# Softmax sums of ten late couples moved in front of the next couple's scores, with undivided x

## The chip, the core and the metric

The kernel runs on one core of a Trainium2 chip. The core has four engines that compute and that run beside each other, each in its own order: TensorE (PE) for matrix products, VectorE (DVE), ScalarE (ACT) and GpSimd (POOL). A fifth, SyncE (SP), issues most of the transfers. PE writes into PSUM, a small memory of eight banks; DVE and ACT empty it into SBUF, the working memory. The metric is the time of one execution on the device in microseconds (us), the median of several runs.

## What is computed

An attention block over 8 batches and 12 heads (448 rows of 64), with q and k normalised by their root mean square, and behind it a feed-forward block with a silu:

```python
q_n, k_n = (rmsnorm(q, g_q), rmsnorm(k, g_k))
scores = scale * np.matmul(q_n, k_n.transpose(0, 1, 3, 2))
scores = scores - np.max(scores, axis=-1, keepdims=True)
attn = np.exp(scores)
attn = attn / (np.sum(attn, axis=-1, keepdims=True) + 1e-09)
attn_out = np.matmul(attn, v).astype(np.float32)
...
x = np.ascontiguousarray(attn_out.transpose(0, 2, 1, 3)).reshape(B * S, H * D)
h = x @ w_in
g = h * (1.0 / (1.0 + np.exp(-h)))
return (g @ w_out).astype(np.float32)
```

All of it is in fp32. The sum of the exponentials (the softmax sum) and the product with v are independent of each other: the division may be done on the result, x.

## The kernel before

The function `bounded` holds the path that these inputs take. Work is cut into 24 couples: a couple is four heads of one batch, that is two pairs of heads, and three couples make a batch. `GROUP` is 6 (two batches), `LATE` is 9 and `SOON` is 11; `FULL` names couples 6 and 10, whose sums have an additional term. The order of all instructions is written out by hand; there is no scheduler that reorders them. Semaphores make one engine wait for another, and a tile pool makes the first writer of a buffer wait for the last reader of its former content.

For each couple c there are two stretches.

`visit(c)` computes the transposed scores of couple c, seven times four matmuls of 64 rows and 64 columns on four tiles of the PE array at once (L749). ACT takes each bank through exp into `weights` (L754). Between the scores stand the products of weights with v (`weigh`, L786): those of the last key block and of the left-over keys of couple c-1 first, then those of couple c. They accumulate in two banks, `av0` and `av1`, of which there is one buffer each. When couple c-1 is complete, `divide` (L855) multiplies each bank by the reciprocal softmax sums on DVE and writes x to SBUF. Only then can PE begin on av for couple c. `turn` (L762) is a copy of one column that orders the two halves of `weigh`; PE waits for it.

`between(c)` runs the first feed-forward product for a group of batches that is complete (`halves_in`, L955): products after Strassen and Winograd, seven for each block of 2 by 2, each of three matmuls of 128 x 128. A matmul of fp32 shows as two passes in the trace. `fill` deals them out: a call has a due number of matmuls (14 in the late couples), and other work is put between them. Items of `others` are spread evenly over the steps; items of `prompt` go in at the start and then after every third step. A between has two fills. The first one carries `late`, the adds of the couple's weights into one block (`add`, L800, on DVE) among others. Ahead of the second fill stands `sum_up`: four matmuls with a matrix of ones, on tiles of 128 rows and 32 columns (L824, eight passes), write the softmax sums into a bank. Then `prompt` holds `invert` of its left half, `invert` of its right half with `spread`, and the transposing of k (`flip`, L685, and `gain`). `invert` (L833) is a reciprocal on DVE from PSUM into `r`; `spread` copies it (L839) and lets SP issue four small transfers that exchange the halves of partitions (L842).

Banks: products take turns between the pool of `mm` (two buffers) and that of `sc` (two buffers of two banks). `sc` also serves the scores, `sum_up` from couple 6 on, and L715, a small product at the end of between whose result DVE (L716) and POOL (L719, L728) turn into the factors for q. A product that is begun in one fill can be completed in the next between; it then keeps its buffer of `mm` through the visit.

When a group of six couples is complete, its x is summed in pairs (`sum_x`), and the products of that group run in the betweens of the next six couples. The last group's products and the second feed-forward product follow after couple 23, where PE has no attention work.

Of the kernel before, what the change touches and what calls it, by code (L numbers as in the profile page):

```python
# [11 lines left out]
F32 = mybir.dt.float32  # L12
# [15 lines left out]
BANK = 512  # L28
# [514 lines left out]
def bounded(  # L543
# [3 lines left out]
    P, D, R, J, S = z.P, z.D, z.R, z.J, z.S  # L547
# [9 lines left out]
    GROUP, LATE = z.NPAIR, z.LATE  # L557
    EARLY = GROUP - 1
    SOON = 2 * GROUP - 1
    FULL = (GROUP, SOON - 1)  # L560


    hidden = dram.tile([z.NF, P, z.B * S], F32, name="hidden")
# [67 lines left out]
    def x_of(c, i):  # L631
        b, cp = divmod(c, z.NPAIR // 2)
        return xT(b, 2 * cp + i)
# [75 lines left out]
    def scale(c):  # L709

        if c >= NC:
            return
        f = norm.rms[c % 2][:, 0:n]
        t = ps.tile([P, 2, BANK], F32, name="sc", bufs=2)[:, 0, 0:n]
        nc.tensor.matmul(t, ident, f, start=True, stop=True)  # L715
        nc.vector.tensor_scalar(  # L716
            out=f, in0=t, scalar1=1.0 / D, scalar2=1e-6, op0=ALU.mult, op1=ALU.add
        )
        nc.gpsimd.tensor_tensor(out=f, in0=f, in1=minus_half.to_broadcast([P, n]), op=ALU.pow)  # L719
        if c > SOON:  # L720
            scale_rows(c, nc.gpsimd)
# [14 lines left out]
    sums = [None] * 2  # L736
# [67 lines left out]
    def sum_up(c):  # L804

        n = D // 2
        early = c < GROUP  # L810
        t = bank(S) if c < GROUP else ps.tile([P, 2, BANK], F32, name="sc", bufs=2)[:, 0, 0:S]
        terms = [(0, lambda: weights(c, 0))]
        if early:
            terms = [(0, lambda: weights(c, LEFT - 1))] + terms + [(1, None)]
        if c in FULL:
            terms.insert(0, (1, None))
        if c == GROUP - 1:
            terms.insert(1, (0, lambda: weights(c, 1)))
        for k, (which, w) in enumerate(terms):
            if early and k == len(terms) - 2:  # L820
                yield
            for h in range(2):
                for i in range(2):
                    nc.tensor.matmul(  # L824
                        t[ds(h * D + i * n, n), :],
                        ones[:, which + i if which else 0],
                        left_weights(c)[:, h] if which else w()[:, i, h],
                        start=(k == 0), stop=(k == len(terms) - 1),
                    )

        def invert(half):
            rows = ts(half, S // 2)
            nc.vector.reciprocal(out=factors(c)[0][:, rows], in_=t[:, rows])  # L833

        def spread():
            mine = [a.rearrange("(h i p) s -> i h p s", h=2, i=2) for a in factors(c)]
            queues = (nc.sync, nc.gpsimd if c == GROUP - 1 else nc.sync)
            if c >= EARLY:
                nc.vector.tensor_copy(factors(c)[1], factors(c)[0])  # L839
                for i in range(2):  # L840
                    for h in range(2):
                        queues[h].dma_start(mine[i][1 - i, h], mine[i][i, h])  # L842
                return
            for h in range(2):
                for i in range(2):
                    nc.sync.dma_start(mine[1][i, h], mine[0][1, h])
            for h in range(2):
                nc.sync.dma_start(mine[0][1, h], mine[0][0, h])

        yield [lambda: invert(0), lambda: (invert(1), spread())]  # L850

    def divide(c, source):
        for i in range(2):
            x = x_of(c, i)
            nc.vector.tensor_tensor(  # L855
                out=x, in0=x if source is None else source[i], in1=factors(c)[i], op=ALU.mult
            )
# [72 lines left out]
    def bank(n):  # L930
        turn = turns["next"] = (turns["next"] + 1) % 4
        due = filler["due"] / S
        if turns["least"] < due <= turns["most"] and not turns["aside"]:
            turns["aside"] = True
            return ps.tile([P, 2, BANK], F32, name="sc", bufs=2)[:, 0, 0:n]
        turns["aside"] = False
        if ps_alone is None or turn == 0:
            return ps_mm.tile([P, BANK], F32, name="mm")[:, 0:n]
        return ps_alone.tile([P, BANK], F32, name="alone")[:, 0:n]
# [536 lines left out]
    def visit(c):  # L1476

        beside = normalise(c + 1) if 0 < c <= GROUP else []
        if c == GROUP:
            beside = [lambda: None] + beside[2:]  # L1480
        if c < NC:
            scores(c, 0, 0)
        for step in visits.get(c, "")[:1]:
            step_of[step]()
        if c == 0:
            first_q(1)
            normalise_alone(1)
            scores(c, 1, 0)
        if c == 0:
            run_all(beside[0:1])  # L1490
        else:
            weigh(c - 1, LEFT)
            weigh(c - 1, LEFT - 1, 0)
            turn(1, nc.scalar.copy if c <= GROUP else nc.vector.tensor_copy)
            run_all(beside[0:1])
            if GROUP < c < NC and c % GROUP == 0:
                sum_x(last_two(c), 0, range(2, 4))
        if c < NC:
            scores(c, 0, 1)
        if c > 0:  # L1500
            weigh(c - 1, LEFT - 1, 1)
            if c - 1 < EARLY:
                for i in range(2):
                    nc.vector.tensor_copy(x_of(c - 1, i), sums[i])
                run_all(beside[1:2])
                if c == GROUP // 2 + 1:
                    divide(c - 2, None)
                if inverting:
                    while len(inverting) > 1:
                        inverting.pop(0)()  # L1510
                    if c > 1:
                        divide(c - 2, None)
            else:
                divide(c - 1, sums)
                if c == GROUP:
                    for i in range(1, HW):
                        sum_x(last_two(c), i, range(2))
                    for i in range(2):
                        norm.scale(c + 1, q_of(c + 1), q_of(c + 1), i, nc.vector)
                    room.w_in.round()  # L1520
                run_all(beside[1:2])
                if GROUP < c < NC and c % GROUP == 0:
                    for i in range(1, HW):
                        sum_x(last_two(c), i)
                weights_in_visit(c)
            if c + 1 < NC:
                loads["vrest"](c + 1)
        if c == NC:
            return
        if c > 0:  # L1530
            scores(c, 1, 0)
        scores(c, 1, 1)
        if c <= GROUP:
            run_all(beside[2:3])
        weigh(c, 0, 1)
        scores(c, 2, 0)
        weigh(c, 1, 1)
        turn(0, nc.scalar.copy)
        if c < GROUP:
            run_all(beside[3:4])  # L1540
        scores(c, 2, 1)
        weigh(c, 0, 0)
        if c < GROUP:
            scores(c, LEFT)
        if c != GROUP - 1:
            run_all(add(c, 1))
        weigh(c, 1, 0)
        if c < GROUP // 2:
            room.w_in.open()
        if c >= GROUP:  # L1550
            scores(c, LEFT)
        if c + 1 < NC:
            loads["v"](c + 1)
        if len(inverting) == 1:
            inverting.pop()()
# [5 lines left out]
    def between(c):  # L1561

        def transposes_and_sums():
            summing = sum_up(c)
            if c < GROUP:
                next(summing)
            if c == GROUP - 1:
                reciprocals = next(summing)
                divide(c - 1, None)
                sum_x([0, 1], 0)  # L1570
                run_all(reciprocals)
                return
            if c < LATE - 1:
                transpose_k(c + 1)
            reciprocals = next(summing)
            if LATE - 1 <= c < NC - 1:
                reciprocals += [lambda: flip(c + 1, "k"), gain]
            if GROUP // 2 < c < EARLY:
                divide(c - 1, None)
            return reciprocals  # L1580
# [28 lines left out]
        if c == GROUP:  # L1609
# [3 lines left out]
            )  # L1613
            late = third + late + fourth
        late += further[2:] if c >= GROUP else further[:2]
        if LATE - 1 <= c < SOON:
            late.insert(len(late) // 2, lambda: load_q(c + 2))
        fill(late)
# [22 lines left out]
                sum_x([c // GROUP * 2, c // GROUP * 2 + 1], 0, range(2))  # L1641
        if c >= LATE - 2:
            scale(c + 2)
        if GROUP <= c < NC - 1:

            nc.scalar.activation(first, minus_half, AF.Exp)
# [1 line left out]
            while rounder.load():  # L1648
                pass

    begun, inverting = {}, []
    load_q(2)
    for _ in range(2):
        room.w_in.load()
# [240 lines left out]
```

## Time and profile before

| what | us |
|---|---|
| median of three runs | 1301.02 |
| the three runs | 1300.94, 1302.18, 1301.02 |
| the profiled execution, by the same clock as the runs | 1300.95 |
| its span, first to last instruction | 1299.1 |
| visit of couple 15 begins, visit of couple 16 begins | 410.34, 443.77 |
| last sum (couple 23) | 699.79 |

The span by engine: PE is shown busy for 1288.5 us (99%), PE's weight loads for 833.8, DVE for 952.4, ACT for 504.0, POOL for 358.4. The groups that bear on the change, over the whole span: the number after x counts the instructions, then come the busy time in us, the mean of one in ns and the idle time of the engine just before them:

```profile
L754 ACT ACTIVATE work<-sc,rms 128x448 f32<-128x448 f32 x318 | 181.9, 635 | 84.7 <-PE sc L749 72.6
L749 PE MATMUL sc<-work 64*64 64x448 f32 x1344 | 165.0, 543 | 1.2 <-ACT work L652 0.7
L800 DVE TENSOR_TENSOR work<-work 128x896 f32<-128x896 f32 (+1 forms) x110 | 117.6, 1099 | 51.1 <-PE av L786 50.6
L786 PE MATMUL av<-work,rows 64*64 64x448 f32 x1272 | 152.3, 540 | 0.3 <-DVE av L762 0.3
```

A line names the line of the code, the engine and the operation, then what is written and what is read. `64*64` is the tile of the PE array. Ends of matmuls are modelled, so that consecutive ones overlap in the listing; starts are exact. An execution of the kernel has about 1.9 us around the span, which the runs' clock counts too.

### The profile page before, as it was taken

The page shows a single profiled execution, that of the slowest core. Times are in us where ns is not written, and L with a number is a line of the kernel's source. Part 1 is how long each engine was busy: PE and PEld are TensorE (multiplying, and loading weights), DVE is VectorE, ACT ScalarE, POOL GpSimd, SP SyncE. Part 2 cuts the span into 40 slices and gives each one's busy share as a digit, 9 for nine tenths or more (in the row PEclk, how much of TensorE's full clock was granted, in tenths as well). Part 3 has the DMA queues.
Part 4 walks back from the last instruction along what each step waited for, and adds up shares of the span by engine and source line. Part 5 has one row for each costly group of instructions (what it writes and reads, how often), then busy time and mean ns, then how long its engine had stood idle before and what let it go on. Part 6 is the DMA issues. An engine that isn't in the chain of part 4 may idle for free.

```text
span 1299.1 us, 19842 instructions
## 1 busy us (share of the span) xinstructions
PE 1288.5 (99%) x7182; PEld 833.8 (64%) x7182; DVE 952.4 (73%) x1650; ACT 504.0 (39%) x880; POOL 358.4 (28%) x221
## 2 busy tenths in 40 slices
PE   9999999999999999999999999999999999999998
PEld 4444444444444444444444455559999999999997
DVE  6899778768555557656544886698978787878785
ACT  7977566645554554544543344310000010000000
POOL 6755454443334334333311344400000000000000
PEclk9999999999999999999999999999999999999999
DMA  8675447444443444443411466312322323131411
GB/s 228 178 188 139 108 124 194 93 93 91 121 92 89 118 93 93 121 92 90 104 51 50 152 200 229 117 61 89 103 90 90 90 89 127 53 131 49 142 37 40
DMA packets 266159, 144.14 MB, mean 111 GB/s; under 512 B 203748, under 2 KB 249956, under 8 KB 266052
## 3 DMA queue, kind: packets, MB, share of 16 engines
q1 hardware_dynamic: 265424, 141.68, 39.6%
q8 instruction: 59, 0.97, 0.3%
q0 software_dynamic: 320, 0.90, 0.2%
q14 instruction: 48, 0.39, 0.1%
q10 hardware_dynamic: 308, 0.20, 0.1%
HBM read 95.36 MB, written 41.29 MB: 105 GB/s over the span
## 4 chain that ended last, share of the span: by engine, by line
PE 96%; DVE 2%; ACT 1%; DMA 1%; issue 0%; POOL 0%; SPq 0%; ACTq 0%; DVEq 0%; POOLq 0%
PE alone L1277 23%; PE mm L955 20%; PE sc L955 11%; PE av L786 10%; PE sc L749 10%; PE mm L1277 8%; PE alone L955 7%; PE alone L1315 2%; PE sc L824 1%; PE mm L824 1%; PE mm L1315 1%; PE sc L642 1%; PE sc L673 0%; DVE work L904 0%; DVE work L800 0%
## 5 line engine op out<-in xcount | busy, mean ns | idle before, releaser
L754 ACT ACTIVATE work<-sc,rms 128x448 f32<-128x448 f32 x318 | 181.9, 635 | 84.7 <-PE sc L749 72.6
L749 PE MATMUL sc<-work 64*64 64x448 f32 x1344 | 165.0, 543 | 1.2 <-ACT work L652 0.7
L800 DVE TENSOR_TENSOR work<-work 128x896 f32<-128x896 f32 (+1 forms) x110 | 117.6, 1099 | 51.1 <-PE av L786 50.6
L786 PE MATMUL av<-work,rows 64*64 64x448 f32 x1272 | 152.3, 540 | 0.3 <-DVE av L762 0.3
L955 PE MATMUL mm<-x,W 128*128 128x448 f32 x366 | 150.2, 543 | 0.2 <-DVE stage L904 0.2
L955 PE MATMUL mm<-sums_x,W 128*128 128x448 f32 x348 | 143.1, 543 | 0.0
L503 POOL TENSOR_TENSOR rms<-rms,minus_half 128x14 f32<-128x14 f32 (+4 forms) x40 | 95.9, 2401 | 135.4 <-DVE rms L499 132.2
L530 POOL DMA_DIRECT2D out_dram<-x x2 | 1.2, 592 | 443.3 <-DVE x L904 443.3
L955 PEld LDWEIGHTS mm<-x,W 128*128 128x128 f32 x366 | 68.1, 190 | 72.3 <-issue 66.9
L1277 PE MATMUL alone<-W,rows 128*128 128x192 f32 x610 | 113.0, 326 | 0.0
L955 PEld LDWEIGHTS mm<-sums_x,W 128*128 128x128 f32 x348 | 64.9, 190 | 69.2 <-issue 65.0
L786 PEld LDWEIGHTS av<-work,rows 64*64 64x64 f32 x1272 | 60.0, 132 | 67.1 <-issue 32.1
L1277 PEld LDWEIGHTS alone<-W,rows 128*128 128x128 f32 x610 | 101.5, 190 | 0.0
L955 PE MATMUL sc<-x,W 128*128 128x448 f32 x246 | 100.1, 543 | 0.0
L749 PEld LDWEIGHTS sc<-work 64*64 64x64 f32 x1344 | 54.9, 132 | 68.0 <-ACT work L754 26.0
L719 POOL TENSOR_TENSOR rms<-rms,minus_half 128x28 f32<-128x28 f32 x15 | 72.2, 4814 | 64.0 <-DVE rms L716 64.0
L978 POOL TENSOR_TENSOR parts<-parts,stage 128x448 f32<-128x448 f32 x31 | 43.1, 1389 | 151.1 <-DVE parts L904 150.2
L955 PEld LDWEIGHTS sc<-x,W 128*128 128x128 f32 x246 | 46.0, 190 | 48.9 <-issue 45.8
L1277 PE MATMUL alone<-W,work 128*128 128x192 f32 x382 | 72.2, 326 | 0.0
L1287 ACT COPY rows<-alone 128x192 f32<-128x192 f32 x33 | 10.5, 318 | 142.1 <-PE alone L1277 142.1
L1108 ACT ACTIVATE stage<-stage 128x896 f32<-128x896 f32 x63 | 57.0, 945 | 17.7 <-DVE stage L904 17.1
L1277 PEld LDWEIGHTS alone<-W,work 128*128 128x128 f32 x382 | 63.8, 190 | 0.0
(265 smaller groups left out, 2290.6 us busy)
## 6 DMA issues: line engine op xcount, KB each, us to landing
hidden<-stage SPq DMA_DIRECT2D x63, 448.0 KB, 2.8
work<-hidden SPq DMA_DIRECT2D x21, 1024.0 KB, 5.1
rows<-in_moe_w_out_dram SPq DMA_DIRECT2D x32, 384.0 KB, 3.6
W<-in_moe_w_in_dram SPq DMA_DIRECT2D x22, 512.0 KB, 5.3
x<-hidden SPq DMA_DIRECT2D x7, 1024.0 KB, 5.4
rows<-in_q_dram SPq DMA_DIRECT2D x120, 56.0 KB, 2.2
rows<-in_k_dram SPq DMA_DIRECT2D x120, 56.0 KB, 2.3
rows<-in_k_dram SPq DMA_DIRECT2D x60, 96.0 KB, 2.6
```

The costliest lines, as they stand in the source:

```text
L503: nc.gpsimd.tensor_tensor(out=t, in0=t, in1=half, op=ALU.pow)
L719: nc.gpsimd.tensor_tensor(out=f, in0=f, in1=minus_half.to_broadcast([P, n]), op=ALU.pow)
L749: nc.tensor.matmul(two[ds(half * D, D), h, 0:S], keys[rows, ts(half, D)], qT[rows, pair, :], start=True, stop=True,)
L754: nc.scalar.activation(left_weights(c)[:, h] if j == LEFT else weights(c, j)[:, i, h], two[:, h, 0:S], AF.Exp, scale=norm.column(c, i, h, j),)
L786: nc.tensor.matmul(sums[i][ds(h * D, D), :], v, w, start=(j == 0 and step == 1), stop=(j == LEFT - 1 and step == 1),)
L800: nc.vector.tensor_tensor(out=total, in0=total, in1=more, op=ALU.add)
L824: nc.tensor.matmul(t[ds(h * D + i * n, n), :], ones[:, which + i if which else 0], left_weights(c)[:, h] if which else w()[:, i, h], start ...
L955: nc.tensor.matmul(t, self.left(name, s), self.right(name, s), start=s == ends[0], stop=s == ends[1])
L978: nc.gpsimd.tensor_tensor(out=u2, in0=u2, in1=p5, op=ALU.add)
L1108: nc.scalar.activation(t, t, AF.Silu)
L1277: nc.tensor.matmul(t, x[:, i], y, start=i == ORDER[0], stop=i == ORDER[-1])
L1315: nc.tensor.matmul(o, a[:, 2 * i + m, t], right_one(name, i)[:, m], start=n == 0, stop=n == len(steps) - 1,)
```

## The change

`LAGGED` names ten couples: 12 to 16 and 18 to 22. For these the call of `sum_up` moves from the middle of between(c), ahead of the second fill, to its end, behind L715 and in front of the next visit's scores. It writes into a buffer of `mm` in place of `sc`. The two steps that `sum_up` hands back wait in the list `lagging`: the first reciprocal is issued in visit(c+1) behind the first scores, the second one, with `spread`, behind the place where x is emptied. There, x is copied from the banks as it is. It is multiplied by the reciprocals in SBUF one between later: as first item of `prompt` in between(c+1), or, where couple c+1 is not in the list (17 and 23), as last item of `late` in the first fill. The items of `prompt` keep their places, with empty steps where the reciprocals were.

```diff
     FULL = (GROUP, SOON - 1)
+    LAGGED = [c for c in range(SOON + 1, NC) if c % GROUP != GROUP - 1]
...
         n = D // 2
         early = c < GROUP
-        t = bank(S) if c < GROUP else ps.tile([P, 2, BANK], F32, name="sc", bufs=2)[:, 0, 0:S]
+        if c < GROUP:
+            t = bank(S)
+        elif c in LAGGED:
+            t = ps_mm.tile([P, BANK], F32, name="mm")[:, 0:S]
+        else:
+            t = ps.tile([P, 2, BANK], F32, name="sc", bufs=2)[:, 0, 0:S]
...
         for step in visits.get(c, "")[:1]:
             step_of[step]()
+        if lagging:
+            lagging.pop(0)()
...
             else:
-                divide(c - 1, sums)
+                if lagging:
+                    for i in range(2):
+                        nc.vector.tensor_copy(x_of(c - 1, i), sums[i])
+                    lagging.pop(0)()
+                else:
+                    divide(c - 1, sums)
...
         def transposes_and_sums():
+            if c in LAGGED:
+                first = [lambda: divide(c - 1, None)] if c - 1 in LAGGED else [lambda: None]
+                return first + [lambda: None, lambda: flip(c + 1, "k"), gain]
             summing = sum_up(c)
...
         late += further[2:] if c >= GROUP else further[:2]
+        if c - 1 in LAGGED and c not in LAGGED:
+            late.append(lambda: divide(c - 1, None))
...
         if c >= LATE - 2:
             scale(c + 2)
+        if c in LAGGED:
+            lagging.extend(next(sum_up(c)))
...
-    begun, inverting = {}, []
+    begun, inverting, lagging = {}, [], []
```

## The prediction

> **What bounds the kernel now.** I read the chain of waits first, then who waited for whom on TensorE (PE), then the timeline of PE alone in the stretch of the ten couples (300 to 700 us), then that of VectorE (DVE) beside it.
>
> ```profile
> PE 96%; DVE 2%; ACT 1%; DMA 1%; issue 0%; POOL 0%; SPq 0%; ACTq 0%; DVEq 0%; POOLq 0%
> ```
>
> The chain lies on PE for 96% of the span; the list of waits of PE has one entry between 308 and 712 us, 0.3 us long. So PE is never idle by the page, and a gain must be a slot of PE that gets shorter. Busy time can't show that, because the ends of matmuls are modelled; their starts can. PE alone, from one between (couple 15) into the next visit (couple 16); columns are start, length, line, tile, count:
>
> ```profile
> 430.43 1.67 PE L955 MATMUL mm<-x,W 128*128 128x448 f32 x4
> 432.03 0.96 PE L824 MATMUL sc<-work,ones 128*32 128x448 f32 x8
> 432.92 1.02 PE L955 MATMUL mm<-x,W 128*128 128x448 f32 x2
> 433.77 2.42 PE L955 MATMUL sc<-x,W 128*128 128x448 f32 x6
> 436.03 2.42 PE L955 MATMUL mm<-sums_x,W 128*128 128x448 f32 x6
> ...
> 443.54 0.30 PE L715 MATMUL sc<-rms,ident 128*128 128x28 f32 x2
> 443.77 0.98 PE L749 MATMUL sc<-work 64*64 64x448 f32 x8
> 444.58 1.68 PE L786 MATMUL av<-work,rows 64*64 64x448 f32 x16
> ```
>
> Six passes of a product take 436.03 - 433.77 = 2.26 us, 0.376 each: that is the floor. Eight passes on four tiles take two floors, 0.752. The softmax sum (L824, tiles of 128*32) cuts into the stream of 128*128 products: the four passes ahead of it take 1.60 (floor 1.504), its own eight 0.89 (0.752), the two behind it 0.85 (0.752). The excursion costs 0.10 to leave, 0.14 inside, 0.10 to come back. The visit also begins with a switch, to 64*64: L715, then scores in 0.81 where later ones take 0.75. How the switch from 128*32 to 64*64 looks is in the trace too, early on, where sums already stand in front of scores:
>
> ```profile
> 38.85 0.94 PE L824 MATMUL mm<-work,ones 128*32 128x448 f32 x8
> 39.72 0.98 PE L749 MATMUL sc<-work 64*64 64x448 f32 x8
> 40.52 0.93 PE L786 MATMUL av<-work,rows 64*64 64x448 f32 x8
> ```
>
> The scores behind the sums take 0.80 there, as behind L715.
>
> Two sums have a larger slot. Couples 22 and 23, PE:
>
> ```profile
> 666.15 1.25 PE L824 MATMUL sc<-work,ones 128*32 128x448 f32 x8
> 667.33 1.02 PE L955 MATMUL sc<-x,W 128*128 128x448 f32 x2
> ```
>
> ```profile
> 699.79 0.94 PE L824 MATMUL sc<-work,ones 128*32 128x448 f32 x2
> 701.00 0.95 PE L824 MATMUL sc<-work,ones 128*32 128x448 f32 x6 [0.27 <-DVE work L800]
> 701.88 1.77 PE L955 MATMUL mm<-sums_x,W 128*128 128x448 f32 x4
> ```
>
> 1.18 and 2.09 us where the others take 0.89: 0.29 and 1.20 of waiting for the last add of weights (L800). DVE at couple 23:
>
> ```profile
> 699.20 0.62 DVE L904 TENSOR_TENSOR stage<-mm,stage 128x448 f32<-128x448 f32 x1 [2.90 <-issue]
> 699.86 1.09 DVE L800 TENSOR_TENSOR work<-work 64x896 f32<-64x896 f32 x1
> ```
>
> The add stands behind an evacuation that could only start when its product ended at 698.94. From about 717 us to the end the starts lie at the floor, so time won before is passed on whole.
>
> **What the Trainium skill says.** "TensorEngine Tiling (Array Packing)", Key Properties: changing the tiling mode drains the engine; the trace agrees, 0.33 us for an excursion of two switches. "Perfetto Trace Analysis", Tensor Engine Instruction: the end of a matmul is estimated, not observed; the trace agrees (2.42 us shown, next start after 2.26), which is why I use starts. "VectorE: DVE Perf Modes", Why PSUM operands drop a tier: from PSUM an fp32 copy is no faster than a two-input operation; the trace agrees, L1504 616 ns and L855 from PSUM 620. "GPSIMD Engine Reference", Key points: POOL shares SBUF interfaces with DVE operations of two SBUF inputs; the ten L855 from SBUF take 560 to 1465 ns, those from PSUM 614 to 626.
>
> **The change part by part.**
>
> *The sums move.* Ten couples (12 to 16, 18 to 22). Removed each time: the leaving and the return, 1.60 + 0.85 - 6 x 0.376 = 0.19. Kept: the sum's own 0.89. At the new place L715 has left 128*128 anyway, and the scores start as in the early case. 10 x 0.19 = 1.9 us, nothing beside it, as PE sets the end. With it goes couple 22's 0.29: its adds are long done by the end of between.
>
> *Couple 23 keeps its sum,* but its list of late work grows from four items to five (the multiply of couple 22). The planner deals item k at step 14k/n: the last add moves from step 14 to step 12 of 14, ahead of the evacuation that is issued with step 14. The order of the changed kernel shows it on DVE: both 64x896 adds, then L904, then the two multiplies. The add then ends near 697.4, and PE needs it at 699.79: 1.20 goes. Late next there: nothing on PE (0.10 to leave and 0.14 stay). Couple 17 gets an item too, but its sum had no wait (0.89).
>
> *The bank.* The sum now takes a buffer of mm (two of them) instead of sc. In front of visits 13, 16, 19 and 22 one product is begun and holds the other buffer, so the sum needs the buffer of the product before it, which ends 0.75 + 0.23 us ahead. DVE there:
>
> ```profile
> 443.05 0.62 DVE L904 TENSOR_TENSOR stage<-mm,stage 128x448 f32<-128x448 f32 x1 [2.30 <-ACT stage L1108]
> ...
> 446.33 0.16 DVE L762 COPY av<-minus_half 128x1 f32<-128x1 f32 x1 [2.26 <-PE av L786]
> 447.83 1.16 DVE L855 TENSOR_TENSOR x<-av,work 128x448 f32<-128x448 f32 x2 [1.34 <-PE av L786]
> 453.44 2.09 DVE L800 TENSOR_TENSOR work<-work 128x896 f32<-128x896 f32 x2 [4.46 <-PE av L786]
> ```
>
> It is empty at 443.67, and the sum could start at 443.77: 0.10 to spare, against 0.05 that a release takes (L800 ended at 700.95, PE went on at 701.00). Bounds 0 and 0.1 in each of four visits; I take 0.1 in all. Before the other visits the buffer is empty 0.7 us or more ahead. In the next between the first mm product needs the begun product's evacuation, ready 0.8 us ahead at the tightest (490.53 against 491.34).
>
> *Reciprocals in the visit.* Two L833 of 1.54 and the copy L839 (0.39 to 1.12). The first stands in DVE's queue ahead of L762, which PE waits for. PE's sum takes 443.77 to 444.66, so the reciprocal runs about 444.85 to 446.4; L762 is wanted at 446.33 + 0.89 = 447.2: 0.8 to spare. The second stands behind the two copies that free av: begun at 447.83 + 0.89 = 448.72, after 1.16 + 1.54 + 0.39 (1.12 at worst) DVE is free at 451.8 (452.5), and the adds come at 454.3. So the idle 2.26 and 4.46 hide them; without that cover each us would count ten times.
>
> *Empty undivided.* Copies for multiplies: 616 against 620 ns, nothing. The multiplies (L855 from SBUF, 1.2 to 2.9 us a pair) go to the head of the second fill, where 3.5 to 4.2 us of reciprocals and copy went away: DVE is freer there, and evacuations come no later.
>
> *Queues.* SP: the four DMAs of spread (L842) move from between into the visit, in front of the loads of v's last keys (L325, L327), which go out some 3 us later and are first used a visit (33 us) later. They no longer stand in front of the k loads (L255) and the saves of hidden. POOL's order is unchanged; ScalarE's (ACT's) differs in one place (couple 17). The multiply comes over 10 us after spread is issued (a fill of 14 matmuls of 0.75 us lies between); spread's issue takes 2.5.
>
> Sum: 1.9 + 0.3 + 1.2 - 0.1 = 3.3 us. The profiled execution took 1300.95 with a span of 1299.1, so 1297.65 and a span of 1295.8; the median of the runs lies 0.07 above the profiled one: 1297.7.
>
> **The rivals.** *Only the switches:* couple 23's wait has another end than the add, or comes back at the next product; -1.9 - 0.3 + 0.1, so 1298.9 us. For: that wait is one event in one execution. Against: L824's first tiles started at 699.79, the rest 0.05 after the add. *Nothing arrives:* a later stage hides the gain, or each switch costs as much at the new place; 1301.0. For: DVE is busy to about 80% after 900 us. Against: PE's starts at the floor there, and the early sums. *Slower:* the reciprocals hold up DVE in the visit, L762 or the emptying of av comes late, and PE stands still. It decides from the point where the first reciprocal starts 0.8 us later than worked out; if a whole reciprocal too many came in front of the copies, 1.54 - 0.8 = 0.74 in ten visits, 7.4 - 3.3 = 4.1 us more: 1305.1. For: DVE works in order, and L855 ends at 448.99, 0.1 us before PE wants av again (449.10). Against: the order puts the second reciprocal behind the copies.
>
> **How the numbers follow.** Forecast 0.70, only the switches 0.16, nothing 0.07, slower 0.07. A measurement of this kernel tells about 0.2% (2.6 us) from no change. The forecast's own range is 1296.6 (small stalls at the end of visits, about 0.1 us in each of ten, go too) to 1298.3. The two cases without the full gain and the scatter of the runs (1.2 us) carry the upper end to 1300.0; below, 1296.3. Faster: the forecast and a fifth of the second case, 0.73; same 0.20; slower 0.07.
>
> **What would show it.** Right: L824 to L749 in 0.89, L749 in 0.80, no L824 between L955 except at couples 17 and 23; 23's slot 0.89; period of a couple 33.44 down to 33.25. Wrong: L824 starting over 0.1 us after L715's slot ends; waits of PE for L762 or for the copies; a wait for L833.

## The result and the profile after

| | before | after |
|---|---|---|
| median of the runs, us | 1301.07 (10 runs, 1300.69 to 1302.18) | 1297.91 (10 runs, 1297.36 to 1299.61) |
| ratio after to before, with its 95% interval | | 0.9976 [0.9966, 0.9986] |
| span of the profiled execution, us | 1299.1 | 1295.9 |

The kernel became 3.2 us faster; 1297.7 was forecast, and for the span 1295.8. In the changed code the lines have moved by one to six: sum L830, scores L750, turn L763, weigh L787, adds L801, reciprocal L839, its copy L845, spread's transfers L848, multiply L861, evacuation L910, products L961. New is L1524, the copy of x from its banks.

The chain of waits on the page of after can't be set beside that of before. Its shares add up to 65% (PE 64%, DVE 1%): the walk back breaks off, so this is a hole in the view and no sign that PE waits for a third of the time. What decides is again the starts on PE. First the place in couple 15's between where the sum stood before, inside the fifth product (timeline of PE: start, length, line, tile, count):

```profile
429.93 2.42 PE L961 MATMUL mm<-x,W 128*128 128x448 f32 x6
432.19 2.42 PE L961 MATMUL sc<-x,W 128*128 128x448 f32 x6
```

The six passes that the sum cut into four and two now take 2.26 us, and nothing cuts in. Then the same sum at its new place, in front of couple 16's visit:

```profile
441.21 0.92 PE L961 MATMUL mm<-sums_x,W 128*128 128x448 f32 x2
441.96 0.30 PE L716 MATMUL sc<-rms,ident 128*128 128x28 f32 x2
442.38 0.96 PE L830 MATMUL mm<-work,ones 128*32 128x448 f32 x8
443.26 0.98 PE L750 MATMUL sc<-work 64*64 64x448 f32 x8
```

From the sum to the scores it is 0.88 us, and the scores take 0.81. L716 to the sum is 0.42, where 0.23 would do: that is a wait, to which we come. In eight other visits it is 0.23; in front of couple 23's visit there is no L716, and the sum follows the products directly. The end of couple 23's first fill, PE and then DVE:

```profile
697.83 0.96 PE L830 MATMUL sc<-work,ones 128*32 128x448 f32 x8
698.72 1.77 PE L961 MATMUL mm<-sums_x,W 128*128 128x448 f32 x4
```

```profile
693.28 2.19 DVE L801 TENSOR_TENSOR work<-work 64x896 f32<-64x896 f32 x2
697.25 0.62 DVE L910 TENSOR_TENSOR stage<-mm,stage 128x448 f32<-128x448 f32 x1 [1.77 <-issue]
```

The last adds are done 1.8 us before the evacuation starts, and the sum's slot is 0.89 in place of 2.09. DVE in the visit of couple 16:

```profile
443.40 1.56 DVE L839 RECIPROCAL work<-mm 128x224 f32<-128x224 f32 x1 [0.92 <-PE mm L830]
445.82 0.16 DVE L763 COPY av<-minus_half 128x1 f32<-128x1 f32 x1 [0.86 <-PE av L787]
447.32 1.16 DVE L1524 COPY x<-av 128x448 f32<-128x448 f32 x2 [1.34 <-PE av L787]
448.39 1.55 DVE L839 RECIPROCAL work<-mm 128x224 f32<-128x224 f32 x1
...
452.93 2.09 DVE L801 TENSOR_TENSOR work<-work 128x896 f32<-128x896 f32 x2 [2.56 <-PE av L787]
```

In front of L763, of the copies and of the adds DVE still waits for PE (the brackets), and not the other way round: both reciprocals, and the copy L845 behind the second one, are covered.

To compare runs I add up, over all starts of PE from 200 to 720 us, how far each lies behind the floor of 0.376 us a pass, and call the sum the excess. It leaves out the first 200 us, where the loading differs from run to run. In before it is 19.69, in after 16.44: 3.25 less. That is 10 slots of sums at 0.195, couple 22's 0.29 and couple 23's 1.21, less 0.19 of wait at couple 16.

### The profile page after: what moved, and what is told of

Its sections match the earlier page's. It is cut to its first block, busy times and chain, and to the rows that moved or that the text cites. A ratio compares the mean times of both kernels' runs of the same rounds, so it can differ in the third digit from the quotient of the medians.

```text
span 1295.9 us, 19847 instructions
## 1 busy us (share of the span) xinstructions
PE 1286.1 (99%) x7182; PEld 834.8 (64%) x7182; DVE 962.1 (74%) x1670; ACT 503.8 (39%) x880; POOL 359.1 (28%) x221
## 4 chain that ended last, share of the span: by engine, by line
PE 64%; DVE 1%; issue 0%; POOL 0%; ACT 0%; DVEq 0%; ACTq 0%; POOLq 0%
PE alone L1283 23%; PE mm L961 10%; PE mm L1283 8%; PE alone L961 7%; PE sc L961 6%; PE av L787 4%; PE sc L750 3%; PE alone L1321 2%; PE mm L1321 1%; PE mm L830 0%; DVE work L910 0%; DVE x L910 0%; DVE rows L907 0%; PE sc L830 0%; POOL rms L503 0%
## 5 line engine op out<-in xcount | busy, mean ns | idle before, releaser
L750 PE MATMUL sc<-work 64*64 64x448 f32 x1344 | 165.1, 543 | 1.0 <-ACT work L653 0.6
L787 PE MATMUL av<-work,rows 64*64 64x448 f32 x1272 | 152.3, 540 | 0.3 <-DVE av L763 0.3
L961 PE MATMUL mm<-x,W 128*128 128x448 f32 x366 | 149.2, 542 | 0.2 <-DVE stage L910 0.2
L961 PE MATMUL mm<-sums_x,W 128*128 128x448 f32 x348 | 142.6, 543 | 0.0
L801 DVE TENSOR_TENSOR work<-work 128x896 f32<-128x896 f32 (+1 forms) x110 | 118.6, 1108 | 32.3 <-PE av L787 31.8
L503 POOL TENSOR_TENSOR rms<-rms,minus_half 128x14 f32<-128x14 f32 (+4 forms) x40 | 96.6, 2418 | 139.0 <-DVE rms L499 135.9
L961 PEld LDWEIGHTS mm<-x,W 128*128 128x128 f32 x366 | 68.4, 190 | 70.9 <-issue 64.2
L961 PEld LDWEIGHTS mm<-sums_x,W 128*128 128x128 f32 x348 | 65.0, 190 | 68.4 <-issue 62.8
L787 PEld LDWEIGHTS av<-work,rows 64*64 64x64 f32 x1272 | 60.0, 132 | 67.3 <-issue 32.7
L750 PEld LDWEIGHTS sc<-work 64*64 64x64 f32 x1344 | 54.8, 132 | 74.4 <-ACT work L755 26.0
L961 PE MATMUL sc<-x,W 128*128 128x448 f32 x246 | 99.7, 541 | 0.0
L984 POOL TENSOR_TENSOR parts<-parts,stage 128x448 f32<-128x448 f32 x31 | 43.1, 1390 | 152.4 <-DVE parts L910 152.4
L961 PEld LDWEIGHTS sc<-x,W 128*128 128x128 f32 x246 | 46.3, 190 | 47.4 <-issue 46.0
```

What stands on the lines that cost most here:

```text
L503: nc.gpsimd.tensor_tensor(out=t, in0=t, in1=half, op=ALU.pow)
L750: nc.tensor.matmul(two[ds(half * D, D), h, 0:S], keys[rows, ts(half, D)], qT[rows, pair, :], start=True, stop=True,)
L787: nc.tensor.matmul(sums[i][ds(h * D, D), :], v, w, start=(j == 0 and step == 1), stop=(j == LEFT - 1 and step == 1),)
L801: nc.vector.tensor_tensor(out=total, in0=total, in1=more, op=ALU.add)
L961: nc.tensor.matmul(t, self.left(name, s), self.right(name, s), start=s == ends[0], stop=s == ends[1])
L984: nc.gpsimd.tensor_tensor(out=u2, in0=u2, in1=p5, op=ALU.add)
```

## The experiments

Nine runs: eight other kernels, and the one after once more (`again`). `fifth` builds on the kernel before, the others on the one after. The table has their medians and the excess, which is that of one traced execution; after and `again`, the same kernel, are 0.44 apart in it.

| kernel | time, us (runs) | ratio to before, 95% interval | excess, us |
|---|---|---|---|
| after | 1297.91 (10) | 0.9976 [0.9966, 0.9986] | 16.44 |
| fifth | 1299.88 (13) | 0.9990 [0.9982, 0.9999] | 18.49 |
| four | 1299.28 (21) | 0.9988 [0.9981, 0.9995] | 18.07 |
| behind | 1298.16 (12) | 0.9980 [0.9971, 0.9988] | 16.86 |
| more | 1298.56 (14) | 0.9982 [0.9974, 0.9990] | 17.46 |
| double | 1302.22 (20) | 1.0008 [1.0001, 1.0015] | 21.22 |
| ahead | 1302.99 (1) | one run | 18.91 |
| direct | 1327.67 (1) | one run | 45.18 |
| pool | 1297.82 (11) | 0.9977 [0.9968, 0.9986] | 16.23 |
| again (after once more) | 1298.21 (14) | 0.9980 [0.9972, 0.9988] | 16.88 |

### Is it the number of late items that freed couple 23?

The theory: the wait for the last add went because the list of late work has five items and the add is dealt two steps earlier. The rival: it went with the moved sums. `fifth` gives the kernel before an empty fifth item, and nothing else:

```diff
         late += further[2:] if c >= GROUP else further[:2]
+        if c == NC - 1:
+            late.append(lambda: None)
```

> The kernel before with one empty item more at the end of couple 23's late work: no sum is moved, and DVE does nothing new. Theory (dealing): with five items the last add is dealt at step 12 of 14 instead of 14, ahead of the evacuation; the slot of couple 23's sum shrinks from 2.09 us to 0.89, all other slots stay: -1.2 us, 1299.85. Rival (only the switches count; the wait of couple 23 comes back elsewhere): 1301.07, the slot or one behind it stays long.

Measured 1299.88, against 1300.95 for the kernel before on that chip. Couple 23's sum in its trace, on PE:

```profile
700.38 0.96 PE L824 MATMUL sc<-work,ones 128*32 128x448 f32 x8
701.27 1.77 PE L955 MATMUL mm<-sums_x,W 128*128 128x448 f32 x4
```

The slot is 0.89 with no sum moved at all. `four` is the reverse: the changed kernel with the list back at four items, the multiply behind the fill:

```diff
-        if c - 1 in LAGGED and c not in LAGGED:
-            late.append(lambda: divide(c - 1, None))
...
         fill(late)
+        if c - 1 in LAGGED and c not in LAGGED:
+            divide(c - 1, None)
```

> The changed kernel, but the multiplies of x of couples 16 and 22 are issued behind the first fill instead of as last item of its late work, so that list has its old length. Theory (dealing): the slot of couple 23's sum is back at about 2.09 us; the ten moved sums keep their gain: +1.2 us on the changed kernel, 1299.1. Rival (the moved sums alone carry the gain): 1297.9 and a slot of 0.89.

Measured 1299.28. The wait is back, as large as before (1.20 of the excess; another 0.24 is the wait of the sum in front of couple 16's visit, 0.42 here in place of 0.19, and 0.2 lies in small places). PE of `four`:

```profile
699.24 0.95 PE L830 MATMUL sc<-work,ones 128*32 128x448 f32 x6 [0.27 <-DVE work L801]
```

So more than a third of what the change brought comes from an item that it put into a list, and could be had with one empty item and no sum moved.

### How much room have the reciprocals in the visit?

`double` computes the first reciprocal twice, so that L763 stands behind 1.5 us more:

```diff
         if lagging:
+            lagging[0]()
             lagging.pop(0)()
```

> The changed kernel with the first reciprocal of each of the ten couples issued twice: 1.54 us of DVE work more, ahead of L762 in DVE's queue. Theory (DVE in the visit has spare time, and only what goes beyond it costs): in the trace of the changed kernel the reciprocal ends 0.86 us before L762 starts, and L762 ends 0.34 before PE's next weighing, 0.05 of which a release takes: 1.15 spare. So 1.54 - 1.15 = 0.39 in each of ten visits: +3.9 us, 1301.8. By the prediction's rule (0.8 spare): +7.4, 1305.3. Rival (DVE in the visit is hidden anyway): 1297.9.

Measured 1302.22. PE, then DVE of `double` at couple 16:

```profile
446.98 0.93 PE L750 MATMUL sc<-work 64*64 64x448 f32 x8
448.08 0.98 PE L787 MATMUL av<-work,rows 64*64 64x448 f32 x8 [0.17 <-DVE av L763]
```

```profile
447.88 0.15 DVE L763 COPY av<-minus_half 128x1 f32<-128x1 f32 x1
```

L763 no longer waits for PE (its bracket is gone), and PE goes on after 1.10 where 0.75 would do. A delay of 1.55 costs 0.35 there, so the room is 1.2 us, not the 0.8 of the prediction. Behind the stop the products take 0.81 where 0.75 would do (448.08 to 448.89), so that the whole visit is 0.40 longer, and 0.40 to 0.43 in all ten. That makes 4.2 of the 4.78 of excess over after; 0.54 is the bank's wait (0.42 at couple 16 in place of 0.19, 0.31 at couple 22).

`ahead` puts the second reciprocal, its copy and the spread ahead of the copies that free av:

```diff
                 if lagging:
+                    lagging.pop(0)()
                     for i in range(2):
                         nc.vector.tensor_copy(x_of(c - 1, i), sums[i])
-                    lagging.pop(0)()
```

> The changed kernel with the second reciprocal, its copy and spread issued in front of the two copies that empty av. Theory: the copies start at 1.54 + 0.39 us behind L762 at the earliest, that is 0.65 later than now, 0.1 is spare: at least 0.5 in each of ten visits, +5 us, 1303; up to 2 us each (1318) if the copy of the reciprocals waits for POOL, which works then. Rival (emptying av is hidden by ACT's lead): 1298.

Measured 1302.99, in one run. That this is the expected number is luck: 2.7 us of it are there before couple 6's visit begins (114.79 against 112.08 in after), where the two kernels do the same. So only the visits are read. From first scores to the first product the visit of couple 16 takes 11.21 us (446.49 to 457.70) against 11.00 in after (443.26 to 454.26): 0.21 more, 0.26 on the mean of the ten visits, not the 0.5 or more expected. The reason stands at the visit's end. There the last scores take 1.07 in after, 0.3 above the floor, and 0.86 in `ahead`. About 0.2 us of what is lost in the middle is thus regained. The place of the second reciprocal behind the copies is right, but the price of the wrong place is small: 2.47 of excess over ten visits.

`direct` takes the undivided copies away: both reciprocals right behind the first scores, and the banks of av are multiplied as in the kernel before.

```diff
-        if lagging:
+        while lagging:
             lagging.pop(0)()
...
-                first = [lambda: divide(c - 1, None)] if c - 1 in LAGGED else [lambda: None]
+                first = [lambda: None]
...
         if c - 1 in LAGGED and c not in LAGGED:
-            late.append(lambda: divide(c - 1, None))
+            late.append(lambda: None)
```

> The changed kernel's sums in front of the scores, but both reciprocals, the copy and spread directly behind the first scores, and x multiplied as it leaves the bank, as before. Theory: the second half of the sums' way (1.54 + 0.39 and four DMAs: 1.9 of issue and 2.0 to landing) ends about 4 us after av should be emptied: PE waits 3.8 to 4.6 us in each of ten visits, 1336 to 1344. Rival (the undivided x is not needed): 1298.

Measured 1327.67, in one run. The visit of couple 16 takes 13.65 (451.82 to 465.47), 2.65 more than in after; eight other visits lose 2.7 to 2.9 and that of couple 17 loses 5.2, in which both multiplies wait for spread's transfers. Over the span it is 30.0. (The 45.18 of the table shows a little less, since at 720 us this kernel is not as far as after.) The multiply of the second bank, DVE of `direct`:

```profile
459.30 0.62 DVE L861 TENSOR_TENSOR x<-av,work 128x448 f32<-128x448 f32 x1 [0.55 <-DMA work<-work]
```

It waits for spread's transfers, and PE waits for av. This is what the copies of x undivided save: without them the moved sum costs more than it gains. The expected time was too high, since spread's transfers go out 3.6 to 5.5 us after the visit's start here and the visit's end gives 0.2 back.

### Where does the bank's wait at couple 16 come from?

The sum in front of couple 16's visit starts at 442.38, behind the evacuation of its bank. DVE of after:

```profile
440.60 1.07 DVE L705 TENSOR_REDUCE rms<-rows 128x28 f32<-128x896 f32 x1
441.70 0.62 DVE L910 TENSOR_TENSOR stage<-mm,stage 128x448 f32<-128x448 f32 x1
```

In front of the visits of couples 13, 19 and 22, where a product is begun too, the evacuation is done 0.10 before the sum's start, as worked out (341.72 + 0.62 against 342.44). What is late only at 16 goes back to SP. What SP issues in couple 15's time, before:

```profile
423.12 3.98 SPq L255 DMA_DIRECT2D rows<-in_q_dram  x8
427.20 0.90 SPq L994 DMA_DIRECT2D hidden<-stage  x2
```

and after:

```profile
416.97 2.48 SPq L848 DMA_DIRECT2D work<-work  x4
...
424.39 5.23 SPq L255 DMA_DIRECT2D rows<-in_q_dram  x8
429.71 0.90 SPq L1000 DMA_DIRECT2D hidden<-stage  x2
```

Counted from the visit's first scores, the save of `hidden` (L1000) goes out at 19.9 us in place of 16.9. Spread waits at the head of SP's queue for the reciprocal's copy, then takes 2.48 us to issue, and all that follows shifts: the loads of v's last keys, of q, and then the save. The loads of q begin 1.8 us later (14.55 after the first scores in place of 12.78); the other 1.2 is that they take 5.23 to issue in place of 3.98, for a reason that the traces don't show. In this couple 15 differs from couple 21: there spread stands in the queue as well, but the loads of q take 4.07, the save goes out at 18.9, and couple 22's visit has no wait. (In front of couples 13 and 19 there is no spread in the queue.) The next writer of the saved buffer is a copy by ACT:

```profile
432.68 0.53 ACT L981 COPY stage<-mm 128x448 f32<-128x448 f32 x1 [5.16 <-DMA hidden<-stage]
```

ACT has been idle for 5.16 us when the save's end releases it. From there the trace leads on through ACT, POOL's power and sum (L503, L984) to an evacuation by DVE and k's transposing behind it (L686, ended at 440.17). Two ways lead from that to L910 at 441.70 and are equally long: DVE's own order, with L705 to 441.67, and a copy by ACT to 441.66. Two experiments test this. `behind` lets spread be issued at the end of the visit, behind the loads of v:

```diff
+        if c in LAGGED:
+            yield [lambda: invert(0), lambda: (invert(1), duplicate()), exchange]
...
         if c + 1 < NC:
             loads["v"](c + 1)
+        if lagging:
+            lagging.pop(0)()
```

(`duplicate` is the copy L845, `exchange` the four transfers.)

> The changed kernel, but the four DMAs of spread are issued at the end of the visit, behind the loads of v; reciprocals and the copy stay. Theory (SP's queue): in the changed kernel the loads of v, the loads of q and the saves of hidden go out 2 to 3 us later than before, because spread waits at the head of the queue for DVE; a buffer of stage is free later, ACT, POOL and DVE follow, and the evacuation in front of visit 16 is 0.19 us late for the moved sum. With spread behind them the save goes out about as early as before and the wait is gone: 0.2 us less, 1297.7, L715's slot at visit 16 back to 0.23. Rival (the wait is the bank's own, from the sum being in mm): the 0.19 stays.

Missed: 1298.16, and the wait at couple 16 is 0.42, which `again` has as well. The trace says why it didn't go: spread's four issues (421.73 to 424.21) still stand ahead of the loads of q, and the save goes out at 20.5 us. Only v's loads had been relieved, and the wait doesn't hang on them. `pool` gives the four transfers of the ten couples to POOL:

```diff
             queues = (nc.sync, nc.gpsimd if c == GROUP - 1 else nc.sync)
+            if c in LAGGED:
+                queues = (nc.gpsimd, nc.gpsimd)
```

> The changed kernel, but POOL issues the four DMAs of spread of the ten couples, at the same place in the visit. In the run 'behind' they still stood ahead of the loads of q and the saves of hidden, so the save of couple 15 went out 20.5 us after the visit's start (before the change 16.9, changed kernel 19.9). Theory (SP's queue): with spread off SP's queue the save goes out at about 16.9 again, ACT's copy behind it at 20.3, and the wait of the sum in front of visit 16 is gone: L715's slot 0.23 there, span 0.2 to 0.4 us shorter, about 1297.7. Rival (the wait comes from the buffer of mm itself): the slot stays at 0.4 to 0.65. POOL is idle at that place, so nothing else moves.

Its save goes out at 16.9 us, as before the change. ACT's copy comes at 21.4 and not at the 20.3 expected, since it still waits for the save's end, but that is early enough. PE in front of couple 16:

```profile
441.88 0.30 PE L716 MATMUL sc<-rms,ident 128*128 128x28 f32 x2
442.12 0.96 PE L830 MATMUL mm<-work,ones 128*32 128x448 f32 x8
```

0.24, no wait, here or at any other couple. The other traces agree: in the six with the wait (after, `four`, `behind`, `more`, `double`, `again`) ACT's copy starts 22.8 to 23.6 us after couple 15's first scores, in the four without it (before, `fifth`, `pool`, and `ahead`, whose spread is released 2.5 us earlier) 20.3 to 21.6. `direct`, whose PE is itself held up in that visit, has its copy at 24.25 and no wait. So the cause is what stands in SP's queue ahead of the save. `again`, the kernel after once more on the same chip, shows the wait with 0.42, and another 0.18 in the two passes ahead of L716:

> The changed kernel once more, for comparison with 'pool' on the same chip: 1297.9, L715's slot in front of visit 16 between 0.4 and 0.65 us in the profile.

The medians are 1297.82 and 1298.21, 0.39 apart, with the runs of both between 1297.2 and 1300.1: the traces resolve the difference, the runs don't. `pool` is the best version that was run, by an amount that the time alone doesn't show.

### Can more sums be moved?

`more` adds couples 8, 9 and 10:

```diff
-    LAGGED = [c for c in range(SOON + 1, NC) if c % GROUP != GROUP - 1]
+    LAGGED = [c for c in range(LATE - 1, NC) if c % GROUP != GROUP - 1]
```

> The changed kernel with three couples more in the list: 8, 9 and 10. Theory (switches): each gains 0.19 us, 0.6 in all: 1297.3. Rival (DVE in the visit): the visits of couples 9, 10 and 11 carry the rounding and the sums of weights and the scaling of q on DVE behind the place where x is emptied; two reciprocals and a copy (3.5 us) in front of them make q's transposing or the weights late, PE waits: 1 us or more slower than the changed kernel.

Measured 1298.56, 0.65 above after and 0.35 above `again`. Three switches should have taken 0.58 off the stretch from 200 to 308 us; its excess rose by about 0.4 instead. PE there:

```profile
209.14 2.52 PE L961 MATMUL mm<-x,W 128*128 128x448 f32 x6 [0.19 <-DVE stage L910]
```

PE waits for an evacuation by DVE that starts at 208.50. In after the same evacuation starts at 208.58 and nothing waits: there PE wants the bank at 209.82, in `more` already at 208.79, because the sum no longer stands in front of these products. In front of couple 10's visit, too, PE arrives earlier and waits longer (L716 for DVE's L705, 0.8 in place of 0.6). So the kernel is a little slower, as the rival said, but by less than its 1 us, and not by its way (data of q or weights that come late behind the reciprocals): there DVE sets the pace, and what PE gains in switches it loses in waits. The bank's wait is also longer at couple 16 (0.27) and new at couple 22 (0.30); whether the early couples have a part in that stayed open.

## Why the prediction was right, and where its terms were off

- *The switches.* 10 x 0.19 were taken, 1.94 measured. The prediction's reason needs a correction: L715 has not left 128*128, its lines show it on that tile; the tile changes behind it. Its slot is 0.23 whether scores or the sum follow, so leaving is paid once, as before. The Trainium skill ("TensorEngine Tiling (Array Packing)", Key Properties) says that a change of tiling mode drains the engine. The trace refines it: returning to 128*128 costs 0.10, while from 128*32 on to 64*64 the scores' slot is 0.80 to 0.81, the same as behind L716's 128*128. So a switch that happens anyway gets no dearer here by the stop at 128*32; only the 0.14 inside the sum stay.
- *Couple 22's 0.29 and couple 23's 1.20.* Measured 0.29 and 1.21; for the latter `fifth` and `four` show the cause from both sides. "Only the switches" falls with this.
- *The bank.* 0.1 in all was taken, 0.19 measured (0.60 in `again`, the same kernel), in one visit and not spread over four. In the three others the working held. The step that failed is the prediction's paragraph on queues: it asked who reads the loads of v that move back (5.7 us, from 4.05 after the first scores to 9.71, not some 3), found no one near, and stopped. Of the saves of `hidden` it said only that spread no longer stands in front of them. In truth that of couple 15 stands farther down the same queue and goes out 3 us later, and it holds a buffer that a chain of ACT, POOL and DVE work needs.
- *Reciprocals in the visit.* Hidden, as forecast; the room is 1.2 us and not 0.8. The forecast let the first one start 0.2 us after the sum's last pass, where 0.14 was seen, and took PE to want L763 when it came before, though PE can take it a little later. The rival "slower" would need over 1.2 us of delay, and a whole reciprocal more on top of the change cost 4.3 us (`double`), so it was farther away than it was put.
- *Emptying undivided.* The copies take 620 ns each as forecast, and the 20 multiplies in SBUF 621 on the mean, the cheap end of the bounds. What the copies save was not in the sum, since they avoid a loss that the change never makes: 2.7 to 2.9 us in nine visits and 5.2 in one (`direct`).
- *Passing on.* In the traces of before and after the excess is smaller by 3.25 at 720 us, and the span by 3.2 at its end: nothing is given back later, and "nothing arrives" falls.

## What to carry to other kernels

When a step moves, list every instruction that its engine issues behind it until the queue runs empty, transfers that write out included, and ask for each who waits for the buffer that it frees; the reader of the load that is moved past is only half of the answer. When work is dealt over steps by its count, adding or taking an item shifts all the others: look at that shift for itself, since it can be had alone. A switch of tiling is best placed where a switch is due anyway. And where another engine sets when a bank comes free, a step saved on PE only brings PE to the wait earlier.

## What the runs showed of the hardware that was not expected

- Four small transfers within SBUF hold SP's queue for 2.48 us after they are released, 0.62 each (2.48 to 3.20 in the ten visits of after), and POOL's for 2.07 in `pool`. While they wait at the head of SP's queue, the loads behind them wait too (9.71 us after the first scores in place of 4.05).
- A visit's last scores have about 0.3 us above the floor, and a delay of PE in the middle of the visit is in part made up there (1.07 to 0.86 in `ahead`; 0.86 in all ten visits of `ahead` and `direct`). Why is not shown.
- The visit of couple 6 begins between 112.03 and 114.79 us in the eleven traces, though all kernels do the same up to there, and two traces of the same kernel are 1.9 apart (112.08 in after, 114.02 in `again`): much of what differs between two executions is made before the work in question begins. A difference of some tenths is better read from the starts behind it than from the medians.
